# A paired tiling for the last 64 inner rows, loads in halves, elementwise work on GpSimd, and a new total order in an SSM-convolution and Mish kernel on one core

## The chip, the core and the metric

The kernel runs on one core of one Trainium2 chip. A core has TensorE (PE, with its weight loads shown apart as PEld), VectorE (DVE), ScalarE (ACT), GpSimd (POOL) and SyncE (SP), which here only issues transfers. The metric is device time in microseconds. Before the change the median of three runs is 235.5 us (234.25 to 236.78).

## What is computed

Sequence length S = 2048, model width D = 640, inner width F = 1728, all in bf16. With x = A_q:

```python
h  = x + A(layernorm(x), A_k, A_v, A_shift_k, A_ssm_k, A_ssm_D)
h2 = h + B(layernorm(h), B_w1, B_b1, B_w2)

def A(q, k, v, shift_k, ssm_k, ssm_D):
    kv = causal_conv(k, shift_k, taps=4) * v        # along S, per channel
    y  = causal_conv(kv, ssm_k)                     # 2048 taps, by FFT in the reference
    return q * (y + kv * ssm_D)

def B(x, w1, b1, w2):                               # 640 -> 1728 -> 640
    return mish(x @ w1 + b1) @ w2
```

## The kernel before

**Layout.** A token's row index is 16 p + a, with p the partition and a = 0..15; "tile t" is the 128 tokens with a = t. The 640 channels are handled as five groups of 128, and these as three chunks: groups 0 and 1 (chunk 0), 2 and 3 (chunk 1), 4 (chunk 2).

**The long convolution** is done by matrix products as a two-stage transform of length 4096. The steps have names, and most of what follows speaks in these names, with the channel group or chunk first and a running number after it:

- `d_n`, `d_k`, `d_v`, `d_g`, `d_x`: loads of A_ssm_k (five of 0.52 MB), A_k (four quarters of 0.66 MB), A_v (two halves of 1.31 MB), the table G (eight blocks of 0.52 MB) and the rows of A_q. `d_id` loads the table `cst`, which holds the identity for transposes and the first transform's cosines and sines.
- `k1pe`, `k1ev`: transposes of A_ssm_k on TensorE and their eviction from PSUM; `dadd` adds ssm_D to the first tap (a row of one partition).
- `s1kpe`, `s1kev` and `s1vpe`, `s1vev`: first transform stage of the filter and of kv, 16 matmuls of 64 columns each, in pairs (cosine L460, sine L461), and the eviction of 1024 columns.
- `ktpe`, `ktev`, `ktsh`: transposes of A_k (each needs one quarter per step; the fourth step of a group needs the last quarter), eviction, and a shift by one on GpSimd; `wsh`: the short convolution's band matrices on GpSimd (L417); `kspe`, `kv`: the short convolution as matmuls and its product with v on VectorE.
- `s2kpe`, `s2kev` and `s2vpe`, `s2vev`: second stage with G, for the filter (22 pieces) and for kv (8, 8 and 4 pieces). `s2kpe` needs every `s1kev`.
- `sw`: copies of the transformed filter with neighbouring partitions swapped, by transfers from the core's memory to itself; each transfer writes 64 of the 128 partitions.
- `p2`, `p1`: the products in the transformed domain, 128x1024 in bf16, on VectorE. `p2` uses the swapped copy.
- `i1pe`, `i1ev`: first inverse stage; `i2pa`, `i2pb`, `i2pc`: second inverse stage of one tile for the three chunks; `y`: its eviction.

**After the transforms**, per tile: `ln1`, `ln1p` and `lnx` normalise x (statistics on VectorE, a power on GpSimd, the scaled row on ScalarE or GpSimd), `wb` multiplies it with y, `h` adds x, `bn` and `pow` are the second statistics, `hc` centres and scales, `trpe` and `trev` transpose it to the channels' side.

**The inner layer** works in five units of 256, 256, 512, 512, 512 tokens. `m1pe` (L780) makes 256 inner rows of a unit as two blocks of 128, 5 matmuls each over the channel groups; `hb` (L788) applies Mish with the bias from PSUM to `hb`. There are 14 blocks of 128 inner rows for 1728 rows: the last one has 64 rows and is filled up with zeros in w1 (`w1z`), and in w2 (`w2z`). `m2pe` (L798) makes one tile's output, two halves of 320 columns with 14 matmuls each, `res` (L805) adds h, `d_out` writes it.

**The order.** One text, `ORDER`, names every step and its engine (t TensorE, a ScalarE, v VectorE, p GpSimd, d a transfer from SyncE). `_schedule` walks through it and gives each step a slot of its rings: four PSUM tiles of 1024 columns (`R_PS`), and rings for row buffers. Each engine then runs its steps in this order, and a step waits on its engine until its inputs and its slot are there. Durations in `_schedule` only decide the merged order of emission and the slots.

Of the kernel before, what the change touches and what calls it, by code (L numbers as in the profile page):

```python
# [10 lines left out]
ACT = mybir.ActivationFunctionType  # L11
# [15 lines left out]
cz:v d_small:p d_id:d d_n2:d wz:v kz:p wm:t cfpe:t coef:v k1pe2:t d_n0:d k1ev2:v d_n1:d wsh3:p dadd2:v d_n3:d k1pe0:t k1ev0:a dadd0:p k1pe1:t  # L27
s1kpe2_3:t s1kev2_3:a s1kpe2_0:t k1ev1:v s1kev2_0:v dadd1:v s1kpe2_1:t s1kev2_1:a s1kpe2_2:t s1kev2_2:a k1pe3:t k1ev3:v d_k0:d s1kpe1_2:t s1kev1_2:a
s1kpe1_0:t s1kev1_0:v s1kpe0_1:t s1kev0_1:a dadd3:p s1kpe0_0:t d_k1:d s1kpe0_3:t s1kev0_3:v s1kev0_0:a s1kpe0_2:t d_n4:d k1pe4:t k1ev4:v d_x0:d
ln1_0:v s1kev0_2:a s1kpe3_1:t wsh2:p s1kpe3_2:t s1kev3_1:a d_k2:d s1kpe1_3:t s1kev3_2:a ktpe0_0:t ktpe0_1:t dadd4:p s1kpe4_0:t s1kev1_3:a s1kev4_0:a  # L30
s1kpe4_1:t ln1_3:v ktpe0_2:t ln1p3:p wsh0:p d_k3:d s1kev4_1:a ktpe0_3:t ktev0:v s1kpe4_2:t wsh1:p d_v1:d s1kev4_2:a s1kpe4_3:t s1kev4_3:v s1kpe3_3:t
s1kev3_3:a ktsh0:p ln1_1:v d_g2:d s1kpe1_1:t s1kpe3_0:t ktpe1_0:t s1kev3_0:a ktpe2_0:t d_g1:d ktpe1_1:t s1kev1_1:a ln1_2:v ktpe2_1:t ktpe1_2:t d_g5:d
ktpe2_2:t ktpe4_0:t d_g3:d ktpe1_3:t ktev1:v ktpe2_3:t ktev2:a ktpe4_1:t ktpe3_0:t ktpe4_2:t ktsh2:p ktpe4_3:t ktev4:v ktpe3_1:t s2kpe_7:t s2kev_7:a
ktpe3_2:t s2kpe_4:t d_g0:d s2kev_4:a d_a12:d ktpe3_3:t ktev3:v s2kpe_6:t ktsh3:p ktsh1:p d_g4:d kspe0_1:t s2kev_6:a kv0_1:v s2kpe_9:t s2kpe_3:t
kspe3_1:t kv3_1:v s2kev_9:a d_v0:d s2kev_3:a d_g7:d d_g6:d s2kpe_14:t s2kev_14:a kspe2_1:t kv2_1:v s2kpe_13:t s2kev_13:a s2kpe_1:t s2kev_1:a kspe1_1:t
kv1_1:v s2kpe_8:t kspe0_0:t kv0_0:v s2kev_8:a s2kpe_11:t s2kev_11:a s2kpe_0:t s2kev_0:a kspe1_0:t s2kpe_15:t s2kev_15:a kv1_0:v kspe4_1:t kv4_1:v
s2kpe_17:t s2kev_17:a s1vpe0_0:t s1vev0_0:a s1vpe0_2:t ktsh4:p s1vpe1_1:t s2kpe_5:t s1vev0_2:v s2kpe_2:t s1vev1_1:v kspe2_0:t kv2_0:v s2kev_5:a
s2kpe_10:t s2kev_2:a s2kev_10:a sw0_0:d s2kpe_12:t kspe4_0:t s2kev_12:a kv4_0:v s2kpe_18:t s2kev_18:v s2kpe_20:t s2kev_20:a s1vpe2_1:t s1vev2_1:a
kspe3_0:t s2kpe_21:t s2kev_21:a s2kpe_19:t kv3_0:v s2kev_19:a s2kpe_16:t s1vpe1_3:t s1vev1_3:a ln1p0:p s1vpe1_2:t sw1_0:d s1vpe1_0:t s2kev_16:v
s1vev1_0:a s1vpe4_3:t s1vev4_3:a s1vev1_2:v ln1p2:p s1vpe0_1:t s1vev0_1:v s1vpe0_3:t s1vpe3_1:t s1vev3_1:v s1vev0_3:a s1vpe3_3:t s1vev3_3:a s1vpe2_2:t  # L40
s1vev2_2:v s1vpe3_2:t s1vev3_2:a sw0_1:d s2vpe0_1:t s2vpe0_0:t s2vev0_0:v s2vev0_1:a p2_0_1:v p2_0_0:v s2vpe0_2:t s2vev0_2:a s1vpe2_3:t s1vev2_3:a
p2_0_2:v sw1_1:d s2vpe0_3:t s2vev0_3:a s1vpe2_0:t s1vev2_0:a s1vpe3_0:t s1vev3_0:v sw2_1:d s2vpe0_5:t p1_0_2:v s2vpe0_7:t p2_0_3:v s2vpe1_3:t p1_0_1:v
s1vpe4_2:t s1vev4_2:v s2vev0_5:a s2vpe0_6:t s2vev1_3:a s2vev0_7:a p1_0_3:v s2vev0_6:a s1vpe4_0:t s1vev4_0:a s2vpe1_7:t s2vev1_7:a p1_0_0:v s1vpe4_1:t
s1vev4_1:a d_t2m:d s2vpe1_4:t s2vpe1_5:t sw2_0:d s2vpe0_4:t p2_0_7:v p2_0_5:v s2vpe1_0:t s2vev1_5:a s2vev1_0:a p1_0_7:v s2vpe1_6:t s2vev1_6:a p1_0_5:v
s2vev0_4:v s2vev1_4:a s2vpe2_3:t s2vev2_3:a p2_0_6:v s2vpe1_1:t p2_0_4:v p2_1_0:v p1_0_4:v p1_0_6:v p2_1_5:v s2vev1_1:a p2_1_3:v s2vpe1_2:t p2_1_7:v
p2_1_1:v s2vev1_2:a p2_1_2:v s2vpe2_0:t s2vev2_0:a i1pe0_7:t p2_1_6:v i1pe0_0:t i1ev0_0:a s2vpe2_1:t p1_1_1:v p2_1_4:v p1_1_0:v p1_1_5:v p1_1_2:v
p1_1_7:v p1_1_3:v s2vev2_1:a p1_1_4:v p1_1_6:v i1pe0_1:t s2vpe2_2:t d_w12:d i1ev0_7:a d_w13:d i1pe0_5:t i1ev0_1:a i1ev0_5:a p2_2_3:v d_w10:d d_x2:d
p2_2_1:v s2vev2_2:a p2_2_0:v i1pe0_3:t i1pe0_2:t i1ev0_2:a i1pe0_6:t i1ev0_6:a p2_2_2:v p1_2_0:v p1_2_2:v i1pe0_4:t d_w14:d i1ev0_4:a p1_2_1:v
i1pe1_0:t d_w11:d d_w2:d p1_2_3:v w2z:p ln1_15:v i1ev0_3:a ln1p15:p i1ev1_0:a ln1_11:v i1pe1_2:t i1ev1_2:a i1pe1_6:t gate:p lnx3:p i1ev1_6:a i1pe1_7:t
lnx2:p i1pe1_1:t i1pe1_5:t i1ev1_1:a i1ev1_5:v i1ev1_7:a i1pe2_2:t i1ev2_2:a i1pe1_3:t i1ev1_3:a i1pe2_3:t i1ev2_3:a i1pe1_4:t i1ev1_4:a i1pe2_1:t  # L50
# [12 lines left out]
d_out0:d h15:v bn15:v pow15:p i2pb13:t trpe8:t ln1p13:p trev8:v i2pc13:t y13:a m2pe6:t trpe10:t bn14:v pow14:p lnx13:a wb13:v m2pe7:t hc9:v hc11:v
# [784 lines left out]
```

## Time and profile before

| | |
|---|---|
| runs (three) | 234.25, 235.5, 236.78 us |
| profiled execution | 234.49 us, its span 232.7 us |
| mean granted TensorE clock | 0.996 |
| TensorE busy | 220.3 us, 2772 matmuls |
| VectorE busy | 145.7 us, 297 instructions |
| ScalarE busy | 141.2 us, 190 instructions |
| GpSimd busy | 42.9 us, 82 instructions |
| moved by DMA | 28.64 MB, 123 GB/s in the mean |

The span runs from the first to the last instruction; the profiled execution's own time is 1.8 us longer. A matmul's duration in the profile contains its way through the array (a 128-column one is shown with 0.219 us where the next one starts 0.055 us later), so work on TensorE is counted by the distance of starts, not by durations. Line numbers are those of the kernel printed above.

### The profile page before, as it was taken

To read this page: it belongs to the slowest core of one execution; us is meant where nothing else is said; L and a number is where in the kernel's file an instruction comes from. 1 tells how busy PE (TensorE), PEld (TensorE's weight loads), DVE (VectorE), ACT (ScalarE), POOL (GpSimd) and SP (SyncE) were. 2 spreads that over 40 slices of the span, in tenths; PEclk is the share of its full clock that TensorE was granted. 3 is DMA by queue.
4 is the path that set the end of the run, shared out by engine and by line. 5 is a ranking of instruction groups with operands and counts; after the bars stand their busy time and mean duration, and the time that the engine had idled before them with its cause. 6 is when DMAs were issued, how large, how long until landed. Compare 5 with 4: busy or idle time off the path is not lost.

```text
span 232.7 us, 6388 instructions
## 1 busy us (share of the span) xinstructions
PE 220.3 (95%) x2772; PEld 168.4 (72%) x2778; DVE 145.7 (63%) x297; ACT 141.2 (61%) x190; POOL 42.9 (18%) x82
## 2 busy tenths in 40 slices
PE   7898999999888999899999999999999999999993
PEld 2897999998778999689787644677654444677771
DVE  0777978898999995889899679688420000102221
ACT  2498999999999999899961457321307378200000
POOL 3443650000100009214313152231000000000000
PEclk9999999999999999999999999999999999999998
DMA  6999992099991999000000000010300000000312
GB/s 191 373 348 411 412 416 86 4 269 278 267 274 16 341 384 347 28 4 0 3 0 3 30 0 0 3 58 0 116 28 0 0 3 0 0 3 0 111 41 74
DMA packets 19022, 28.64 MB, mean 123 GB/s; under 512 B 1137, under 2 KB 15410, under 8 KB 18610
## 3 DMA queue, kind: packets, MB, share of 16 engines
q1 hardware_dynamic: 18880, 28.23, 34.8%
q8 instruction: 21, 0.34, 0.6%
q14 instruction: 7, 0.06, 0.1%
q0 software_dynamic: 64, 0.00, 0.0%
q10 hardware_dynamic: 50, 0.01, 0.0%
HBM read 20.37 MB, written 2.62 MB: 99 GB/s over the span
## 4 chain that ended last, share of the span: by engine, by line
PE 78%; DMA 7%; DVE 6%; ACT 5%; issue 2%; SPq 1%; ACTq 0%; DVEq 0%
PE ps L798 26%; PE ps L780 26%; ACT uv L367 5%; DMA ra<-in_A_k_dram 4%; PE ps L654 4%; PE ps L653 4%; PE ps L566 3%; DMA rn<-in_A_ssm_k_dram 3%; PE ps L602 2%; PE ps L490 2%; PE ps L751 2%; PE ps L460 2%; PE ps L513 2%; PE ps L713 2%; DVE uk L369 1%
## 5 line engine op out<-in xcount | busy, mean ns | idle before, releaser
L780 PE MATMUL ps<-G 128*128 128x512 bf16 (+1 forms) x344 | 62.3, 336 | 0.3
L798 PE MATMUL ps<-rn,uv 128*128 128x320 bf16 x448 | 62.3, 299 | 0.0
L798 PEld LDWEIGHTS <-uv 128*128 128x128 bf16 x448 | 43.6, 98 | 16.9
L788 ACT ACTIVATE uv<-ps,b1s 128x512 bf16<-128x512 f32 (+1 forms) x70 | 37.2, 604 | 26.1 <-PE ps L780 25.4
L780 PEld LDWEIGHTS <-G 128*128 128x128 bf16 x350 | 33.9, 98 | 24.8 <-issue 0.2
L367 ACT CAST uk<-ps 128x1024 bf16<-128x1024 f32 (+2 forms) x54 | 49.5, 1030 | 3.2 <-PE ps L461 1.9
L805 DVE TENSOR_TENSOR xb<-ps,xb 128x640 bf16<-128x640 f32 x6 | 4.8, 821 | 45.3 <-PE ps L798 45.3
L367 ACT CAST uv<-ps 128x1024 bf16<-128x1024 f32 x30 | 28.2, 1076 | 0.5 <-PE ps L461 0.5
L653 PE MATMUL ps<-a,uv 128*128 128x128 bf16 x160 | 18.3, 219 | 0.0
L653 PEld LDWEIGHTS <-uv 128*128 128x128 bf16 x160 | 17.8, 113 | 0.0
L738 POOL TENSOR_TENSOR r<-ve,mhalf 128x1 f32<-128x1 f32 x16 | 9.0, 565 | 39.1 <-DVE ve L735 39.1
L602 PE MATMUL ps<-uv,G 128*128 128x64 bf16 (+1 forms) x384 | 13.4, 187 | 2.8 <-ACT uv L367 1.5
L692 POOL TENSOR_TENSOR r<-ve,mhalf 128x1 f32<-128x1 f32 x16 | 8.9, 558 | 36.7 <-DVE ve L688 36.7
L602 PEld LDWEIGHTS <-G 128*128 128x128 bf16 x384 | 12.1, 96 | 4.0 <-issue 3.0
L519 DVE TENSOR_TENSOR ra<-ps,rb 128x1024 bf16<-128x1024 f32 x10 | 12.2, 1224 | 1.7 <-PE ps L514 1.7
L369 DVE CAST uv<-ps 128x1024 bf16<-128x1024 f32 x10 | 11.9, 1219 | 1.3 <-ACT uv L367 0.9
L617 DVE TENSOR_TENSOR uv<-uv,uk 128x1024 bf16<-128x1024 bf16 x20 | 12.7, 682 | 0.0
L460 PE MATMUL ps<-cst,ra 128*64 128x128 bf16 x160 | 11.0, 220 | 0.6 <-issue 0.5
L367 ACT CAST rb<-ps 128x640 bf16<-128x640 f32 x13 | 8.4, 705 | 5.2 <-PE ps L713 5.1
L367 ACT COPY G<-ps 128x640 bf16<-128x640 bf16 x7 | 4.9, 693 | 10.9 <-PE ps L751 10.9
L566 PE MATMUL ps<-uk,G 128*128 128x160 bf16 x128 | 11.3, 230 | 0.0
L461 PE MATMUL ps<-cst,ra 128*64 128x128 bf16 x160 | 11.2, 221 | 0.0
(104 smaller groups left out, 354.5 us busy)
## 6 DMA issues: line engine op xcount, KB each, us to landing
G<-tab_g SPq DMA_DIRECT2D x8, 512.0 KB, 11.5
rn<-in_A_ssm_k_dram SPq DMA_DIRECT2D x5, 512.0 KB, 6.3
ra<-in_A_k_dram SPq DMA_DIRECT2D x4, 640.0 KB, 8.3
rb<-in_A_v_dram SPq DMA_DIRECT2D x2, 1280.0 KB, 11.3
G<-in_B_w_dram SPq DMA_DIRECT2D x5, 432.0 KB, 7.2
rn<-in_B_w_dram SPq DMA_DIRECT2D x1, 2080.0 KB, 12.2
rn<-uk SPq DMA_DIRECT2D x4, 512.0 KB, 5.2
rb<-uk SPq DMA_DIRECT2D x8, 256.0 KB, 5.2
```

The source lines that it names most:

```text
L367: nc.scalar.copy(o, i)
L369: nc.vector.tensor_copy(o, i)
L460: nc.tensor.matmul(ps[0:64, dgl, :], lhs, mc, start=True, stop=True)
L461: nc.tensor.matmul(ps[64:128, dgl, :], lhs, ms, start=True, stop=True)
L519: nc.vector.tensor_tensor(kv_w[:, m, :, 8 * h:8 * h + 8, :], rt.tile.rearrange("p (l t d) -> p d t l", l=4, t=8), raw_v[:, 8 * h:8 * h + 8 ...
L566: nc.tensor.matmul(ps[:, o:o + 160], g_v[:, f, :], KA[:, :, f, :], start=True, stop=True)
L602: nc.tensor.matmul(ps[:, fl * st:fl * st + n], g_v[:, f0 + fl, :], V[c.i][:, :, f0 + fl, :], start=True, stop=True)
L617: nc.vector.tensor_tensor(v, v, K[c.i][:, :, f0:f1, :], ALU.mult)
L653: nc.tensor.matmul(pz[:, dgl, :], V[c.i][:, dg // 4, :, dg % 4], a12[:, 0, :], start=True, stop=False)
L780: nc.tensor.matmul(ph[:, i * 512:i * 512 + w], w1[:, dc, fc * P:fc * P + P], lnhT_of(u)[:, dc, 0:w], start=(dc == 0), stop=(dc == NDC - 1))
L788: nc.scalar.activation(hb_of(u)[:, fc, 0:w], rt.tile[:, i * 512:i * 512 + w], ACT.Mish, bias=b1s[:, fc:fc + 1], scale=1.0)
L798: nc.tensor.matmul(po[:, a * 512:a * 512 + 320], hb_of(u)[:, fc, tl * P:(tl + 1) * P], w2[:, fc, a * 320:a * 320 + 320], start=(fc == 0), ...
```

## The change

The order is a new one throughout: every engine gets its steps in another sequence. Its beginning, the part around the second stage, and its end:

```diff
-cz:v d_small:p d_id:d d_n2:d wz:v kz:p wm:t cfpe:t coef:v k1pe2:t d_n0:d k1ev2:v d_n1:d wsh3:p dadd2:v d_n3:d k1pe0:t k1ev0:a dadd0:p k1pe1:t
...
+cz:v kz:p wz:v wm:t d_off:d d_n2:d d_n1:d warm:a d_id:a k1pe2:t k1ev2:v dadd2:v cfpe:t k1pe1:t k1ev1:a d_n0:d k1pe0:t coef:v k1ev0:v s1kpe2_2:t
+dadd0:p s1kev2_2:v d_n4:d d_k2:d s1kpe2_1:t dadd1:p s1kev2_1:a s1kpe2_3:t s1kev2_3:a k1pe4:t s1kpe1_3:t s1kev1_3:a k1ev4:v s1kpe1_0:t s1kev1_0:v
...
+s1kev4_0:v s1kev0_2:a d_k0:d dadd3:p s1kpe3_1:t s1kev3_1:a s1kpe3_2:t s1kev3_2:a s1kpe3_3:t s1kpe3_0:t s1kev3_0:a ktpe3_0:t ktpe3_1:t ln1_3:v d_g1:d
+d_k3:d ktpe3_2:t s1kev3_3:v ktpe2_0:t d_g4:d ktpe3_3:t ktev3:v d_g3:d ktpe2_1:t s2kpe_21:t d_g0:d s2kpe_7:t ktpe2_2:t ktpe2_3:t ktev2:v s2kev_21:a
...
-m2pe14:t res14:v d_out14:d res12:v d_out12:d d_out10:d m2pe9:t res9:v d_out9:d m2pe8:t res8:v d_out8:d d_out11:d m2pe13:t res13:v d_out13:d
...
+d_out10:d resa15:v d_outa15:d m2pe8:t res8:v d_out8:d d_out9:d m2pe13:t res13:v d_out13:d m2pe12:t res12:v d_out12:d res11:v d_out11:d d_out1:d
+m2bpe15:t resb15:v d_outb15:d
```

In the new order A_ssm_k's blocks come as 2, 1, 0, 4 ahead of all else on SyncE, then A_k's third quarter, G's blocks 7 and 2, A_ssm_k's block 3, and the other quarters of A_k with G's block 1 between them. All first-stage products of the filter stand ahead of the transposes of A_k. `warm`, which loads the table for Mish, stands at the start of ScalarE's order, ahead of the load of `cst`, which ScalarE now issues. GpSimd has the steps `p2_0_3`, `p2_0_1`, `p1_0_7`, five `wb`, nine `h`, fifteen of the sixteen `hc`, and eight `lnx` instead of six. Up to the first w1 product 13 tiles of the second inverse stage stand on TensorE; before it was 11 and two of the three parts of a twelfth. The rest of the diff, cut:

```diff
     def emit_small(e):
-        nc.sync.dma_start(cst[:], dram["cst"])
+        nc.scalar.dma_start(cst[:], dram["cst"])
...
-        for _ in range(10):
+        for _ in range(9):
             nc.tensor.matmul(ps[:, 0:512], wz[:, 0:P], wz[:, P:D], start=True, stop=True)
...
     def emit_small2(e):
-        nc.gpsimd.memset(b1b[:], 0.0)
         nc.gpsimd.dma_start(b1b[0:13, :], B_b1[0:13 * P].rearrange("(c p) -> c p", p=P))
-        nc.gpsimd.dma_start(b1b[13:14, 0:64], B_b1[13 * P:FF].rearrange("(c p) -> c p", c=1))
+        for o in (0, 64):
+            nc.gpsimd.dma_start(b1b[13:14, o:o + 64], B_b1[13 * P:FF].rearrange("(c p) -> c p", c=1))
...
     def emit_kn(b):
-        return lambda: nc.sync.dma_start(raw_n[b], A_ssm_k.rearrange("(d m l) s -> m d l s", m=NDC, l=4)[b])
+        v = A_ssm_k.rearrange("(d m l) s -> m d l s", m=NDC, l=4)[b]
+
+        def fn():
+            for d in range(0, 32, 16):
+                nc.sync.dma_start(raw_n[b][4 * d:4 * d + 64], v[d:d + 16])
+        return fn
...
             def fn(e, f0=f0, f1=f1, c=c, which=0):
+                eng = nc.gpsimd if e == "pool" else nc.vector
                 v = V[c.i][:, :, f0:f1, :]
                 if which == 0:
-                    nc.vector.tensor_tensor(v, v, K[c.i][:, :, f0:f1, :], ALU.mult)
+                    eng.tensor_tensor(v, v, K[c.i][:, :, f0:f1, :], ALU.mult)
                     return
...
-    w1_z = OP("w1z", ("pool", 0.4), s2_pes + s2k_pes, emit=lambda e: nc.gpsimd.memset(w1[:, :, FF:FP], 0.0), prio=6)
...
-        nc.sync.dma_start(w2[0:64, 13, :], B_w2[13 * P:FF, :])
-    w2_z = OP("w2z", ("pool", 0.6), i1_pes[0], emit=lambda e: nc.gpsimd.memset(w2[64:P, 13, :], 0.0), prio=7)
+        for i in range(2):
+            nc.sync.dma_start(w2[64 * i:64 * i + 64, 13 + i, :], B_w2[13 * P:FF, :])
+    def emit_w2z(e):
+        nc.gpsimd.memset(w2[64:P, 13, :], 0.0)
+        nc.gpsimd.memset(w2[0:64, 14, :], 0.0)
...
         def wbf(e, lnx_rt=lnx_rt, tt_rt=tt_rt):
-            nc.vector.tensor_tensor(tt_rt.tile, tt_rt.tile, lnx_rt.tile, ALU.mult)
+            (nc.gpsimd if e == "pool" else nc.vector).tensor_tensor(tt_rt.tile, tt_rt.tile, lnx_rt.tile, ALU.mult)
...
                 for i in range(2):
                     fc = fp * 2 + i
+                    if fc == NFC - 1:
+                        for dc in range(NDC):
+                            for o in (0, 64):
+                                nc.tensor.matmul(ph[o:o + 64, 512:512 + w // 2], w1[:, dc, fc * P:FF], lnhT_of(u)[:, dc, o * w // P:(o + 64) * w // P],
+                                                 start=(dc == 0), stop=(dc == NDC - 1))
+                        continue
...
+                    n = w // 2 if fc == NFC - 1 else w
+                    nc.scalar.activation(hb_of(u)[:, fc, 0:n], rt.tile[:, i * 512:i * 512 + n], ACT.Mish, bias=b1s[:, fc:fc + 1], scale=1.0)
...
-                        nc.tensor.matmul(po[:, a * 512:a * 512 + 320], hb_of(u)[:, fc, tl * P:(tl + 1) * P], w2[:, fc, a * 320:a * 320 + 320],
+                        o = tl * P
+                        x = 1 if fc == NFC - 1 and o >= w // 2 else 0
+                        nc.tensor.matmul(po[:, a * 512:a * 512 + 320], hb_of(u)[:, fc, o - x * w // 2:o - x * w // 2 + P], w2[:, fc + x, a * 320:a * 320 + 320],
                                          start=(fc == 0), stop=(fc == NFC - 1))
...
+            for a in range(2):
+                o_pe2 = OP(f"m2{'ab'[a]}pe{t2}", ("pe", 1.905), hbs + [d_w2, w2_z, o_pe2], allocs=[] if a else [rt], uses=[rt] if a else [], emit=(lambda e, f=pe2, a=a: f(e, cols=(a,))), prio=100 + u + 0.5)
```

`h` and `hc` get the same choice of engine as `wb`. For the last 64 inner rows, the first half of a unit's tokens now goes to partitions 0 to 63 of the block and the second half to partitions 64 to 127, each with half as many columns; w2 holds the last 64 rows twice, once over zeros and once under zeros, and the bias of these rows is loaded twice. The second product keeps its 28 matmuls of 320 columns per tile. Only tile 15 is cut: `m2ape15` makes its left 320 columns, four tiles run, and `m2bpe15` makes the right ones, with a residual and an output each. `_schedule`'s own durations and waits change too, which moves nothing by itself.

## The prediction

> **What bounds the kernel now.** I read the busy table by slices first, then the work of each engine in stretches of 10 us, then the order of time on ScalarE and on the weak places, and last the chain of waits from 100 us on.
>
> ```profile
> PE   7898999999888999899999999999999999999993
> DVE  0777978898999995889899679688420000102221
> ACT  2498999999999999899961457321307378200000
> DMA  6999992099991999000000000010300000000312
> ```
>
> One digit is 5.8 us. TensorE (PE) is near full everywhere, ScalarE (ACT) only up to slice 16, the DMA engines up to slice 6. Stretches (start:end, then busy us and count of PE, PE weight loads, DVE, ACT, POOL, then clock, DMA share, GB/s):
>
> ```profile
> 20.00:30.00 10.00, 8.65 (x184) 8.21 (x179) 8.28 (x17) 8.73 (x10) 5.96 (x6) 1.00 1.02 411
> 60.00:70.00 10.00, 8.46 (x238) 7.57 (x235) 9.92 (x17) 10.00 (x12) 0.63 (x1) 1.00 0.94 268
> 70.00:80.00 10.00, 8.98 (x220) 8.98 (x219) 10.00 (x24) 10.00 (x12) 0.00 (x0) 1.00 0.48 155
> 100.00:150.00 50.00, 49.89 (x383) 35.54 (x383) 42.55 (x123) 32.90 (x60) 15.11 (x30) 1.00 0.02 5
> ```
>
> So there are three stages. Up to about 29 us the loads bind. From there to 93 us it is ScalarE: in order of time its evictions run from 29.74 to 92.97 us with four pauses, 0.26, 0.16, 0.46 and 0.27, together 1.15 us, 68 casts at a pitch of 0.92:
>
> ```profile
> 29.74 11.95 ACT L367 CAST uk<-ps 128x960 bf16<-128x960 f32 x13 [0.34 <-PE ps L566]
> 54.91 19.34 ACT L367 CAST uv<-ps 128x1024 bf16<-128x1024 f32 x21 [0.46 <-PE ps L461]
> 79.60 12.09 ACT L367 CAST uk<-ps 128x1024 bf16<-128x1024 f32 x13
> ```
>
> From the first product with w1 at 100.86 us to 228.8 TensorE never stops. Pieces of the chain (start, us, what):
>
> ```profile
> 105.82 2.18 PE ps L780 x20
> ...
> 137.38 2.16 PE ps L780 x10
> ...
> 198.36 30.44 PE ps L798 x224
> 228.82 0.82 DVE xb L805
> ```
>
> A 512-wide matmul thus takes 0.216 us, a 256-wide one 0.109, a tile of the second product 30.44/8 = 3.80.
>
> **The last 64 inner rows.** Per unit, 5 matmuls of full width become 5 pairs of half width, two 64-column tiles side by side. That two such tiles run at once is seen in the transform stage, where a new pair starts each 0.055 us, the time of 128 columns once (128 x 0.216 / 512 = 0.054):
>
> ```profile
> 10.16 0.22 PE L460 MATMUL ps<-cst,x 128*64 128x128 bf16 x1
> 10.16 0.22 PE L461 MATMUL ps<-cst,x 128*64 128x128 bf16 x1
> 10.21 0.22 PE L460 MATMUL ps<-cst,x 128*64 128x128 bf16 x1
> 10.22 0.22 PE L461 MATMUL ps<-cst,x 128*64 128x128 bf16 x1
> ```
>
> A 512 unit saves 5 x 0.108 = 0.54, a 256 unit 5 x 0.0545 = 0.27: 3 x 0.54 + 2 x 0.27 = 2.17 us. Each goes into and out of the narrow tiling, 10 changes; where nothing waits, the next matmul in the trace starts about 0.092 late at such a change (0.08 to 0.11 in some 15 places). 10 x 0.092 = 0.92. Net -1.25, all on the path. The order of the transform stage makes 14 such changes instead of 26, 1.1 us, which I count at nothing, since ScalarE hides it. The shorter activations (0.69 to 0.48) and the second zeroing of w2 lie beside other work; so do one warm-up matmul less (0.43) and the bias loads, three issues of 0.5 to 0.76 on GpSimd's queue, moved behind p1_0_7 and some 20 us ahead of their use.
>
> **Start.** SyncE issues the A_ssm_k halves at once, ten issues for five of 0.55 to 0.70, at 0.33 to 0.7 each (the bounds are the rows of its shortest issues and of the whole loads; it has free time after 3 us, since it then waits for landings); cst goes to ScalarE's queue behind a 1.28 us table load and the 0.2 us warm activation, so at about 2.3 us instead of 0.72; with its 2.2 us to landing it is there at 4.5, and the first transposes run at 5.9 in before. If sharing the engines with the halves eats that 1.4 us, each further 0.1 costs 0.1 there, but 25.5 us below hides it. The other table load, 1.28 at 102 us, goes, where the Mish groups wait 25.4 us for PE anyway: nothing.
>
> **When ScalarE's long stretch begins.** The first s2k product follows the transposes of the last A_k quarter, which PE waited for until 22.15 us. Ahead of that quarter and with it came 6.0 MB; now three blocks of G (g7, g2, g1) come before it, 1.57 MB more. At 0.41 MB/us (20 to 30 us) that is 3.8 us, less 0.4 for the earlier start: 25.5 us. But by then all of the s1k work has been done: 20 groups of 0.44 and five transposes of 1.08 fit into 5.9 to 22, and the last of their evictions, on VectorE behind x0 and two statistics of 1.23, ends near 25.5 too. So s2k evictions start at 26.1 instead of 29.74. ScalarE then has 21 x 0.92 + 0.37 + 47 x 0.925 + one lnx 0.82 = 64.0 us to the last i1 eviction, plus the same pauses, 1.15: 91.25 instead of 92.97, -1.7. Ends: no gain if the pauses double and the start is 27; -4 if the G blocks overlap better.
>
> VectorE's load up to its last product rises by 1.8 us by the rows (three more evictions of 1.14, one more statistic of 1.23, less three products of 0.60 and small ones), and in before it is through at 85.35 after 13 us of waits, 6 us ahead of the last transposes; that is the cover. Late loads: A_v's second-issued half is needed by the sixth kv product at about 39 us and ends at 12.3 MB; the last G block (12.85 MB) is used by s2k_15 at 26.1 + 0.4 + 16 x 0.92 = 41; in before 12.8 MB were in by 36 us. The swap copies wait for the eighteenth s2k eviction, 26.1 + 16.5 = 42.6, and went out at 45.6; a12 and t2m, now behind them all, are used after 65 us. The three products given to GpSimd: 128x1024 at the rate of L417 (2058 ns for 1120) 1.88, at that of the copy L499 (608 ns for 508) 1.23; I take L417, also two-input. The three run beside PSUM evictions, which GpSimd does not disturb (L369's 1.22 us copy at 7.15, under L417, is as long as any). Without that cover:
>
> ```profile
> 7.09 2.06 POOL L417 TENSOR_TENSOR hc<-cst,coef 128x1120 bf16<-128x1120 bf16 x1 [4.21 <-DVE coef L409]
> ...
> 8.41 0.83 DVE L543 TENSOR_TENSOR x<-x,rn 1x128 bf16<-1x128 bf16 x1
> ```
>
> This VectorE instruction takes 0.21 elsewhere; here it ends 0.09 after GpSimd's does. Two-input work of the two excludes each other. Two memsets of w2 (0.63 each) also stand on GpSimd's queue ahead of the last of the three products, which the first i1 product needs some 8 us later.
>
> **Into the products.** From the last i1 eviction to the first w1 product it was 7.9 us, with PE idle 0.38 and 1.23 in it while the chain y, gate, residual, statistics, pow, centring ran. Now 13 inverse tiles (0.537 each) instead of 11 and 0.8 of a twelfth fill it: the stretch stays about 8, and 1.2 x 0.537 = 0.65 us of work is gone from behind it. -0.65.
>
> **GpSimd in the second half.** It gets 15 centrings (0.87 by L702, the nearest row), 9 residuals and 5 gates (1.18 by L417), 2 more lnx. The tightest place is tile 7: from h3 on GpSimd's queue to hc7 holds 4 two-input steps, 6 pow, 6 centrings, 5 ln1p, 3 lnx: 4.7 + 3.4 + 5.2 + 4.1 + 2.6 = 20 us. Meanwhile PE has 15.1 of first products, 11.4 of second ones, 2.8 of transposes and inverse tiles: 29 us. 9 us of cover; I take nothing, bounds 0 and +3.
>
> **Tail.** The last residual is half as wide: 0.82 to about 0.45. But res12, res11 and then three outputs, at 0.33 each, are now queued ahead of it on VectorE and SyncE inside the last 1.9 us, and a landing takes 1.8. -0.1, bounds -0.4 and +0.6.
>
> **Sum** on the profiled execution (234.49 us, span 232.7, so 1.8 lie around it): -1.7 - 0.65 - 1.25 - 0.1 = -3.7, so 230.8. The median of the runs, 235.5, stands 1.0 above that execution; the same saving from it would be 231.8.
>
> **Rivals.** (1) *The half loads are slow.* Each half reaches 64 partitions. The nearest rows are the swap copies, also 64 partitions each: 268 to 279 GB/s at 94 to 98% busy engines, against 411 for the 128-partition loads; but they read and write the core's memory, so they don't settle it. 2.62 MB of A_ssm_k take 6.4 us at 411, 9.7 at 270, 12.7 if half the partitions give half the rate. The last A_k quarter comes as much later and ScalarE's stretch with it: +3.3, 234.1, or +6.3, 237.1, slower than before. It decides from 3.7 us of delay on, below 260 GB/s. The Trainium skill, "SBUF — State Buffer", section "Can I just issue two DMAs to hit both halves?", says that two transfers into the two partition halves do not add up (+6% over one), and its table has 196 against 328 GB/s; by that ratio the load would take 10.7 and the sum be 235.1. No trace here shows such a pair. (2) *GpSimd's hold on two-input work makes VectorE the bound* in the product stage: 3 x 1.88 waited out in full and 1.8 of load more are 7.4 against 6 us of cover, +1.4, and the same waits make a centring late by the 3 of the bound above: 235.2. Against it stands that each product is placed beside evictions. (3) *The pairs don't run side by side* when they accumulate: 2.17 is lost, 233.0. For it, only that the transform's pairs don't accumulate. (4) *ScalarE starts earlier:* -4 for -1.7, and half of its pauses gone: 230.8 - 2.3 - 0.6 = 227.9. PE's 1.13 us wait at 21 us is for a load alone, which speaks for it.
>
> **Numbers.** Forecast 0.50, 230.8 with 228.5 to 233; rival (1) 0.28; (2) 0.10; (3) 0.05; (4) 0.07. 1% of 234.5 is 2.3, about what a measurement can tell: 232.1 and 236.8 bound "same". Faster: 0.45 of the forecast, 0.02 of (1), 0.02 of (2), 0.01 of (3) and (4) whole, 0.57. Same: 0.05 + 0.13 + 0.04 + 0.03 = 0.25. Slower: 0.13 of (1), 0.04 of (2), 0.01 of (3), 0.18. The range 227 to 237 leaves out some 0.03 below and 0.12 above; the forecast's own is the one given with it.
>
> **What would show it.** s2k evictions on ScalarE from about 26 us, the last i1 eviction near 91, the first w1 product near 99; a paired group of five at 0.54 us plus twice 0.09; GpSimd busy about 80 us (42.9 + 13 + 16.5 + 5.6 + 1.7); no PE pause after the first product. Loads below 300 GB/s before 12 us and an A_k quarter landing after 28 us would show (1). A PE pause on a centring would make the second half's zero wrong.

## The result, and the profile after

| | before | changed |
|---|---|---|
| median of the runs shown beside each other (us) | 236.1 (4 runs, 234.3 to 237.8) | 253.6 (4 runs, 252.9 to 253.7) |
| ratio, 95% interval | | 1.074 (1.065 to 1.082) |
| span of the profiled execution (us) | 232.7 | 251.9 |
| first transposes of the normalised tiles (us) | 98.8 | 105.7 |
| first product with w1 (us) | 100.8 | 109.3 |
| TensorE's last matmul ends, by the distance of starts (us) | 228.6 | 248.3 |
| GpSimd busy (us) | 42.9 | 110.6 |

The kernel became 17 us slower, where 230.8 was forecast. Two executions at a granted clock near 0.6, one of the kernel before and one of a variant, took about 370 us and enter no ratio given here. 8.5 us are lost ahead of the first w1 product and 11.2 behind it. The changed kernel's span in 40 slices of 6.3 us shows where, in the same rows as before, with GpSimd's (POOL) and the granted clock's:

```profile
PE   6997899988779899598978399999997999999994
DVE  0597897889999999787694628413323000101223
ACT  2278799998979988356913134723223457112000
POOL 0080086007900045559989997997964000000000
PEclk9999999999999999889999689999999999999999
DMA  6999991399926992000000000000030000000122
```

Counted from 0, TensorE, which used to be full from slice 17 on, has holes at slices 16 and 22, GpSimd is at seven tenths or more from slice 18 to 28, and behind both holes the clock that TensorE is granted falls. The same by stretches (start:end, then busy us and count of PE, PE weight loads, DVE, ACT, POOL, then clock, DMA share, GB/s):

```profile
60.00:70.00 10.00, 7.59 (x211) 6.50 (x205) 9.93 (x11) 9.57 (x12) 8.99 (x9) 1.00 0.96 286
...
100.00:110.00 10.00, 7.03 (x63) 5.92 (x62) 7.21 (x18) 4.98 (x9) 4.73 (x5) 0.83 0.01 2
110.00:120.00 10.00, 8.76 (x91) 7.39 (x89) 8.05 (x28) 6.14 (x14) 9.40 (x10) 1.00 0.00 0
...
140.00:150.00 10.00, 6.57 (x38) 4.40 (x40) 4.79 (x14) 2.91 (x4) 9.23 (x11) 0.67 0.01 2
```

In the last two of these stretches GpSimd is the busiest engine. The groups of GpSimd (busy us, mean ns of one, then idle time) say with what:

```profile
L759 POOL TENSOR_SCALAR hc<-xa,mv,r 128x640 bf16<-128x640 bf16 x6 | 15.4, 2562 | 0.3
...
L740 POOL TENSOR_TENSOR rb<-rb,ra 128x640 bf16<-128x640 bf16 x5 | 7.2, 1431 | 2.8 <-ACT rb L372 2.8
...
L718 POOL TENSOR_SCALAR ra<-x,r,nmr 128x640 bf16<-128x640 bf16 x3 | 2.6, 876 | 0.0
```

A centring (L759) takes 2.5 us, where the prediction took 0.87 for it, the time of the norm ahead of the gate (L718, in the kernel before L702): the same engine, shape and type, also with two per-partition operands. The row of before is

```profile
L702 POOL TENSOR_SCALAR ra<-x,r,nmr 128x640 bf16<-128x640 bf16 x4 | 3.4, 867 | 0.0
```

The 15 centrings sum to 37.9 us, not 13. TensorE's waits name the same line (engine, line, releaser: total us, times, longest):

```profile
PEld L767 <- POOL hc L759: 14.9, 8, 4.4
...
PE ps L767 <- POOL hc L759: 12.7, 8, 4.3
```

And in the chain of waits (start, us, what) the worst pause, 4.43 us up to 143.38, is four steps of one queue, with a gate of a later tile (`rb`) standing between two centrings (the last of them is tile 7's):

```profile
136.10 2.51 POOL hc L759
138.61 0.53 POOL r L754
139.14 1.36 POOL rb L740
140.50 2.84 POOL hc L759
143.38 0.71 PE ps L767 x5
```

### The profile page after: what moved, and what is told of

Same layout as the page of the kernel before. It is cut to its first block, busy times and chain, and to the rows that moved or that the text cites. A ratio compares the mean times of both kernels' runs of the same rounds, so it can differ in the third digit from the quotient of the medians.

```text
span 251.9 us, 6466 instructions
## 1 busy us (share of the span) xinstructions
PE 224.0 (89%) x2795; PEld 169.6 (67%) x2802; DVE 142.2 (56%) x267; ACT 135.5 (54%) x185; POOL 110.6 (44%) x117
## 4 chain that ended last, share of the span: by engine, by line
PE 38%; DVE 21%; POOL 19%; DMA 11%; issue 7%; ACT 1%; POOLq 1%; SPq 1%; DVEq 0%
PE ps L823 17%; POOL hc L759 10%; PE ps L802 9%; DMA ra<-in_A_k_dram 4%; DVE uv L630 4%; DMA rn<-in_A_ssm_k_dram 4%; PE ps L578 3%; DMA rn<-uk 3%; POOL r L754 3%; DVE rb L740 2%; DVE rn L634 2%; DVE uv L374 2%; PE ps L501 2%; DVE rb L634 2%; DVE st L749 1%
## 5 line engine op out<-in xcount | busy, mean ns | idle before, releaser
L802 PE MATMUL ps<-G 128*128 128x512 bf16 (+1 forms) x318 | 58.2, 336 | 0.7 <-ACT uv L811 0.4
L802 PEld LDWEIGHTS <-G 128*128 128x128 bf16 x325 | 31.3, 98 | 23.3 <-issue 1.1
L829 DVE TENSOR_TENSOR xa<-ps,xa 128x640 bf16<-128x640 f32 x6 | 4.9, 825 | 41.0 <-PE ps L823 41.0
L767 PE MATMUL ps<-cst,hc 128*128 128x128 bf16 x80 | 7.5, 237 | 12.7 <-POOL hc L759 12.7
L829 DVE TENSOR_TENSOR xb<-ps,xb 128x640 bf16<-128x640 f32 (+1 forms) x7 | 4.9, 726 | 20.1 <-PE ps L823 20.1
L767 PEld LDWEIGHTS <-hc 128*128 128x128 bf16 x80 | 5.3, 106 | 15.3 <-POOL hc L759 14.9
L759 POOL TENSOR_SCALAR hc<-xa,mv,r 128x640 bf16<-128x640 bf16 x6 | 15.4, 2562 | 0.3
L759 POOL TENSOR_SCALAR hc<-xb,mv,r 128x640 bf16<-128x640 bf16 x6 | 15.0, 2506 | 0.2
L614 PEld LDWEIGHTS <-G 128*128 128x128 bf16 x384 | 11.5, 96 | 4.6 <-issue 4.4
L708 POOL TENSOR_TENSOR r<-ve,mhalf 128x1 f32<-128x1 f32 x16 | 8.9, 557 | 10.8 <-DVE ve L704 10.8
L374 DVE CAST uk<-ps 128x1024 bf16<-128x1024 f32 x10 | 12.0, 1220 | 0.6 <-PE ps L472 0.3
```

What stands on the lines that cost most here:

```text
L374: nc.vector.tensor_copy(o, i)
L614: nc.tensor.matmul(ps[:, fl * st:fl * st + n], g_v[:, f0 + fl, :], V[c.i][:, :, f0 + fl, :], start=True, stop=True)
L759: (nc.gpsimd if e == "pool" else nc.vector).tensor_scalar(hc_rt.tile, xt(t2), mv2[:, t2, 0:1], r2[:, t2:t2 + 1], ALU.subtract, ALU.mult)
L767: nc.tensor.transpose(pt[:, dc * P:(dc + 1) * P], hc_rt.tile[:, dc * P:(dc + 1) * P], ident)
L802: nc.tensor.matmul(ph[:, i * 512:i * 512 + w], w1[:, dc, fc * P:fc * P + P], lnhT_of(u)[:, dc, 0:w], start=(dc == 0), stop=(dc == NDC - 1))
```

## The experiments

All times are medians beside runs of the kernel before on the same chip, whose medians were 234.7 to 235.0.

**The centring back on VectorE.** In the order, the letter of 15 steps:

```diff
-hc0:p ... hc2:p hc3:p ... hc15:p
+hc0:v ... hc2:v hc3:v ... hc15:v
```

> The changed kernel with its 15 GpSimd centrings back on VectorE, at the same places of the order; nothing else. Theory A: the loss is the centring itself, which GpSimd takes 2.53 us for (0.45 on VectorE), so that TensorE waits 12.7 us for it and is granted a clock of 0.83 and 0.67 after two of the pauses, some 3 us more. Then 253.6 falls to 236 to 241, the pauses ahead of the transposes (L767) shrink below 4 us, GpSimd's busy time falls from 110.6 to about 73, and the first w1 product, at 109.3 now, comes about 2 to 3 us earlier. Theory B (three products on GpSimd hold VectorE up) and theory C (the half loads delay the start) both leave the second half as it is: no less than 250.

Measured 241.7 (241.5 to 242.1), 0.7 above the range given. GpSimd was busy 72.7 us; TensorE's idle time from 100 us to its last matmul fell from 13.4 to 4.4 us, and the first w1 product came 2.4 us earlier. So the centring on GpSimd is 12 us of the loss.

**The centring on GpSimd in another form.**

```diff
-gpsimd.tensor_scalar(hc, x, mean, r, ALU.subtract, ALU.mult)
+gpsimd.tensor_scalar(nmr2, mean, r, -1.0, ALU.mult, ALU.mult)
+gpsimd.tensor_scalar(hc, x, r, nmr2, ALU.mult, ALU.add)
```

> The 15 centrings stay on GpSimd but are written as x times r plus (minus mean times r), the form that the norm ahead of the gate uses on GpSimd at 0.87 us; the product of mean and r is one more 128x1 step of 0.30 ahead of each. Theory A1: it is the form (subtract first, then multiply) that costs 2.53; then each centring with its small step takes 1.17, GpSimd is busy 20 us less (about 90), and the time falls by most of the 12.7 us of pauses, to 240 to 246. Theory A2: what costs is this tile or this place on GpSimd, whatever the form: it stays at 2.5, the small steps add 4.5 us to GpSimd, 254 to 258.

Measured 240.6 (240.3 to 240.9), GpSimd busy 89.9, a centring 0.87. It is the form, not the engine, that cost 13 us (253.6 less 240.6).

**The three products back on VectorE.**

```diff
-p2_0_3:p ... p2_0_1:p ... p1_0_7:p
+p2_0_3:v ... p2_0_1:v ... p1_0_7:v
```

> The three gating products that went to GpSimd are back on VectorE, at the same places of the order. Theory B: one VectorE product took 2.61 us instead of 0.68 beside one of them, another 1.26; VectorE wins 2.5 us of waits and gets 1.8 us of work, and its last product, which ends at 91.5 now, ends 1 to 3 us earlier, with the time at 250.5 to 252.5. Theory A: the second half is untouched and hides nothing of it, so at most that 1 us is seen: 252.5 to 254.

Measured 252.9 (252.7 to 253.0): 0.7 less. The hold that the prediction named is there, in the changed kernel's VectorE in order of time:

```profile
59.57 1.29 DVE L630 TENSOR_TENSOR uv<-uv,uk 128x1024 bf16<-128x1024 bf16 x2
60.77 2.61 DVE L634 TENSOR_TENSOR rn<-rn,uv 128x1024 bf16<-128x1024 bf16 x1
63.31 2.34 DVE L374 CAST uv<-ps 128x1024 bf16<-128x1024 f32 x2
```

One product takes 2.61 instead of 0.68, ending half a microsecond after GpSimd's product, which ran from 60.31 to 62.84; the next held one takes 1.26. But VectorE must do the three itself when it gets them back, 1.8 us, so little was to be won.

**Whole loads.**

```diff
-for d in range(0, 32, 16):
-    nc.sync.dma_start(raw_n[b][4 * d:4 * d + 64], v[d:d + 16])
+nc.sync.dma_start(raw_n[b], v)
```

> The five A_ssm_k blocks are loaded whole (128 partitions each) as in the kernel before, the rest of the change stays. Theory C: between 3 and 12 us the queue moved 234 to 265 GB/s where it later moves 390 to 430; whole loads bring the last A_k quarter in at about 25.5 instead of 27.9 us and the time falls by up to 2.4, to 251.2 to 252.5. If VectorE's products bound that stage instead, the 2.4 us are hidden and the time stays within 0.8 of 253.6, though the quarter lands earlier.

Measured 251.2, but from 249.7 to 253.0. The rate is beyond doubt. Stretches of the changed kernel, then of this one (the last number is GB/s):

```profile
3.00:6.00 3.00, 2.43 (x6) 0.60 (x4) 0.00 (x0) 0.00 (x0) 0.00 (x0) 1.00 1.07 277
6.00:9.00 3.00, 2.75 (x24) 2.48 (x25) 0.83 (x1) 0.00 (x0) 0.00 (x0) 1.00 1.04 254
9.00:12.00 3.00, 2.91 (x48) 2.60 (x48) 1.94 (x7) 1.73 (x1) 0.00 (x0) 1.00 1.02 243
```

```profile
3.00:6.00 3.00, 3.00 (x14) 1.52 (x13) 0.00 (x0) 0.00 (x0) 0.00 (x0) 1.00 1.04 364
6.00:9.00 3.00, 2.63 (x35) 2.32 (x34) 2.10 (x6) 0.49 (x1) 0.00 (x0) 1.00 0.99 392
9.00:12.00 3.00, 3.00 (x74) 2.84 (x72) 2.46 (x3) 2.58 (x3) 0.91 (x3) 1.00 1.00 409
```

With all DMA engines busy in both (the number before the rate), half loads move two thirds as much. In SyncE's order the last A_k quarter landed at 27.8 us in the changed kernel and at 24.5 with whole loads, 3.4 us earlier. What of it reaches the end is less sure: the span of the profiled execution fell by 1.5 us, the median by 2.4. In that profile TensorE's pause at 20.5 us grew to 2.41, the clock was 0.83 from 20 to 30 us, and ScalarE's long stretch began at 28.12 instead of 28.80. At the same mean clock, 0.993, two executions with whole loads took 249.7 and 250.2 us and two of the changed kernel 252.9 and 253.6: 3.3 us, though only two against two.

**All three together** (multiply and add, products on VectorE, whole loads).

> The three repairs together: centring on GpSimd as multiply and add, the three products back on VectorE, whole A_ssm_k loads; the pairs, the tail in halves, GpSimd's gates and residuals and the new order stay. If the three costs lie one after another on the path, 240.6 less 0.7 less 2.4 gives 237.5 (236.5 to 238.5). If they hide each other (theory D: VectorE bounds the stage of the products whatever comes before), 239 to 240.6. Either way it stays above the kernel before by 2 us or more, since VectorE's stretch from its first to its last product remains some 4 us longer than it was.

Measured 237.1 (235.9 to 238.9), ratio 1.010 (1.006 to 1.013). The three costs add up: 253.6 - 13.0 - 0.7 - 2.4 = 237.5. ScalarE's long stretch now begins here (one group of ScalarE in order of time):

```profile
26.49 12.57 ACT L373 CAST uk<-ps 128x320 bf16<-128x320 f32 x14 [0.43 <-PE ps L574]
```

That is the 26.1 of the prediction; in the changed kernel it was 28.80.

**The pairs alone, in the kernel before.** Of the change only the pairs, w2's second copy of the last 64 rows and that of their bias, in the old order:

```diff
+if fc == NFC - 1:
+    for dc in range(NDC):
+        for o in (0, 64):
+            nc.tensor.matmul(ph[o:o + 64, 512:512 + w // 2], w1[:, dc, fc * P:FF], ...)
+    continue
```

> The kernel before with the paired column tiles alone: its own order, loads and engines; last 64 inner rows as two 64-column tiles, the second copy of their rows of w2 and of their bias, zeros beside it. The step of the prediction: -2.17 of matmuls plus 10 changes of tiling at 0.09 make -1.25, so a ratio of 0.995 (0.993 to 0.998), with a paired group of five at 0.67 to 0.76 us, tiling changes included, where five full matmuls take 1.08. If the pairs ran one after another, the group would take 1.26 and the ratio be 1.004.

Measured 234.0, ratio 0.997 (0.994 to 0.9997), where 0.995 was expected; from the first w1 product to the last matmul 126.8 us instead of 127.8. A unit of 512 in TensorE's order of time:

```profile
142.81 2.32 PE L791 MATMUL ps<-G 128*128 128x512 bf16 x10
145.06 0.74 PE L787 MATMUL ps<-G 128*64 128x256 bf16 x10
145.73 1.53 PE L812 MATMUL ps<-rn,uv 128*128 128x320 bf16 x10
```

Ten half-width matmuls from 145.06 to 145.73: 0.67 us from start to next start, so they run side by side, and the group starts 0.09 late (142.81 + 10 x 0.216 = 144.97). 0.76 in all, by the prediction 0.72.

**Three evictions from VectorE back to ScalarE**, beside the three repairs.

```diff
-s2vev1_7:v ... s2vev1_4:v ... i1ev1_3:v
+s2vev1_7:a ... s2vev1_4:a ... i1ev1_3:a
```

> The kernel with the three repairs, and with three of the evictions that the new order gives to VectorE in the product stage (two of the second v transform of chunk 1, one of the first inverse step) back on ScalarE, at the same places of the order. Theory D: from its first product to its last VectorE does seven evictions of 1.15 us, three in the kernel before, and never waits there; without three of them its last product ends 2.3 to 3.4 us earlier, and the time falls by 1.5 to 3 against the kernel with the three repairs. Rival: ScalarE takes 0.92 more for each, 2.8 us, and pauses only 3.6 us in that stage in all, not always where it is needed; then the gain is under 0.7.

Measured 236.7, ratio 1.009 (1.006 to 1.012), against 1.010 without: not to be told apart. VectorE's last product did end 2.4 us earlier (85.9 instead of 88.3), but ScalarE now runs without any pause from 53.95 us on,

```profile
53.95 21.20 ACT L373 CAST uv<-ps 128x1024 bf16<-128x1024 f32 x23 [0.86 <-PE ps L610]
...
77.50 14.15 ACT L373 CAST uk<-ps 128x1024 bf16<-128x1024 f32 x15
```

and its last inverse eviction ends at 93.3 instead of 94.1. The rival was right: ScalarE is full in this stage, and what VectorE gains there it loses in part to two new waits (1.24 and 0.84 us).

**The centring in four forms, by tile.**

```diff
-gpsimd.tensor_scalar(hc, x, mean, r, ALU.subtract, ALU.mult)
+(hc, x, mean, r, ALU.subtract, ALU.mult), (hc, x, -mean, r, ALU.add, ALU.mult),
+(hc, x, r, mean * r, ALU.mult, ALU.subtract), (hc, x, r, -mean * r, ALU.mult, ALU.add)
```

> The changed kernel with the GpSimd centring written in four forms, by tile: as it is (subtract the mean, multiply by r) for tiles 4, 8 and 12 and 0; add minus the mean, multiply by r; multiply by r, subtract mean times r; multiply by r, add minus mean times r. All have two per-partition operands in f32 and the same tile. Theory A1a: a subtraction costs: the first and the third form take 2.5, the others 0.87. Theory A1b: the order costs (another operation than the multiplication first): first and second 2.5, third and fourth 0.87. Theory A1c: only multiply and add is short: 2.5, 2.5, 2.5 and 0.87. The time of this kernel says nothing more: 242 to 252.

GpSimd in order of time, tiles 4 to 7 (subtract then multiply; add then multiply; multiply then subtract; multiply then add):

```profile
127.58 2.51 POOL L763 TENSOR_SCALAR hc<-xa,mv,r 128x640 bf16<-128x640 bf16 x1
...
131.82 0.87 POOL L766 TENSOR_SCALAR hc<-xa,nmr,r 128x640 bf16<-128x640 bf16 x1
...
133.69 2.52 POOL L769 TENSOR_SCALAR hc<-xa,r,nmr 128x640 bf16<-128x640 bf16 x1
...
138.79 0.88 POOL L772 TENSOR_SCALAR hc<-xa,r,nmr 128x640 bf16<-128x640 bf16 x1
```

The subtraction costs it, first or second; the order of the two operations does not matter, and the third and the fourth form have the same operands. The other tiles show the same to 0.02 us.

**The first tiles on VectorE**, beside the three repairs and the three evictions.

```diff
-wb1:p ... hc0:p
+wb1:v ... hc0:v
```

> The kernel with the three repairs and the three evictions on ScalarE, and of GpSimd's work two steps more back on VectorE, at the same places of the order: the gate of tile 1 and the centring of tile 0. Theory E: ahead of the first w1 product TensorE pauses 1.93 us for this chain: the residual of tile 0 on VectorE takes 1.58 instead of 0.48, since GpSimd's gate of tile 1 (1.65) runs beside it, and the centring on GpSimd takes 0.27 + 0.87 against 0.45 on VectorE. Without both, the chain is 1.1 + 0.7 less 0.45 for the gate on VectorE: TensorE's pause falls to 0.4 to 0.8, the first w1 product comes 1.1 to 1.5 us earlier, and so does the end: 235.2 to 235.6. If something else holds the first tiles (the statistics, the power on GpSimd), less than 0.5 is won.

Measured 236.3, ratio 1.007 (1.004 to 1.010). The pause fell from 1.93 only to 1.35 us, the first w1 product came 0.55 earlier: half of theory E's gain or less, and the times (236.7 without this step) are not to be told apart.

**Everything on VectorE**, beside the three repairs and the three evictions.

```diff
-hc0:p ... wb1:p ... h3:p ...
+hc0:v ... wb1:v ... h3:v ...
```

> The kernel with the three repairs and the three evictions on ScalarE, and all centrings, gates and residuals on VectorE, at the same places of the order: GpSimd keeps what it had before the change. Theory F: GpSimd's help in the second half is worth nothing, since VectorE does the same work 3 times as fast (0.45 for 0.87 + 0.28, 0.48 for 1.40) and is 30 of 40 us busy there, while one GpSimd queue makes tiles 4 to 7 late by 1.8 us: the pauses at 98 and at 128 us fall below 0.6 each, and the time to 233.0 to 234.5, below the kernel before. Theory G: VectorE's load (12 us more in its busiest 50) makes new pauses: 236 or more.

Ratio 1.017 (1.011 to 1.023); five executions took 238.0 to 241.4 us, the middle one 238.2. That is slower than the kernel before, against theory F, and than the 236.7 with GpSimd's help. Where the time goes is read from the last run below.

**The kernel before with pairs and tail in halves.**

```diff
-m2pe13:t res13:v d_out13:d
+m2ape13:t resa13:v d_outa13:d m2bpe13:t resb13:v d_outb13:d
```

> The kernel before with the paired column tiles and with its last tile's second product, residual and output in halves of 320 columns; nothing else. From TensorE's last matmul to the end of the span it is 4.1 us in the kernel before and 3.6 in the changed one, so the halves are worth 0.5, not the 0.1 of the prediction; with the pairs' 1.3 by the profile the span is 230.9 (230.4 to 231.4), and the ratio 0.992 to 0.995. If the halves win 0.1 or nothing, the span stays at 231.4 or above.

Ratio 0.994 (0.991 to 0.997), inside the range given but not to be told apart from the pairs alone; the span, 231.9, lies above its range. So nothing is shown to be won by the halves. TensorE at the end:

```profile
223.77 2.20 PE L812 MATMUL ps<-rn,uv 128*128 128x320 bf16 x15
226.55 2.06 PE L812 MATMUL ps<-rn,uv 128*128 128x320 bf16 x14 [0.58 <-DVE xb L817]
```

Between the halves TensorE pauses for the first half's residual. From its end to the span's it is 3.45 us instead of 4.05; the pause of 0.75 takes that back.

**The same with another product between the halves.**

```diff
-m2pe8:t res8:v d_out8:d d_out11:d m2ape13:t resa13:v d_outa13:d m2bpe13:t
+m2ape13:t m2pe8:t resa13:v d_outa13:d res8:v d_out8:d d_out11:d m2bpe13:t
```

> The kernel before with pairs and tail in halves, where the last second product's first half now runs one product earlier (its two halves have the product of tile 8 between them, as the changed kernel has others between them). In the kernel with the halves next to each other TensorE paused 0.75 us at 225.8, behind the first half's residual on VectorE, since both halves lie in one tile of PSUM. Theory H: that pause took back the 0.6 that the shorter tail won (3.45 instead of 4.05 us from TensorE's end to the span's); without it the span is 230.6 to 231.1 and the ratio 0.991 to 0.994. If the halves are worth nothing in themselves, the ratio stays at the 0.997 of the pairs alone.

Measured 233.2, ratio 0.992 (0.988 to 0.996): the lowest median of all kernels here. The pause is gone and TensorE's end is 3.5 us from the span's. The profiled execution itself misses its forecast (233.1): its first half ran about 2 us later, at a clock of 0.97 from 40 to 100 us; the middle span of the twelve executions is 231.4, also a little above the 230.6 to 231.1. The interval overlaps that of the pairs alone, so the half microsecond of the tail rests on the two profiles.

**One gate less on GpSimd**, beside the first tiles' two steps.

```diff
-wb11:p
+wb11:v
```

> The kernel with the first tiles' two steps on VectorE, and of GpSimd's gates one more, that of tile 11, on VectorE too. Theory I: TensorE's pause of 1.75 us at 127 us is the centring of tile 7, which stands on GpSimd's queue behind this gate (1.40), as the centring that took 2.84 stood there at 140 us in the changed kernel. Without it the pause falls to 0.2 to 0.5 and the end comes 1.2 to 1.5 us earlier: 234.8 to 235.2, level with the kernel before. If GpSimd's queue as a whole is what is late (six steps of centring, power and norm before it), another step takes its place and under 0.5 is won.

Measured 234.7, ratio 0.998 (0.995 to 1.002), level with the kernel before, and 1.6 below the kernel without this step, as theory I has it. In the kernel with the three evictions GpSimd's order of time had shown that gate in front of tile 7's centring:

```profile
126.47 1.40 POOL L736 TENSOR_TENSOR rb<-rb,ra 128x640 bf16<-128x640 bf16 x1
127.84 0.61 POOL L756 TENSOR_SCALAR nmr<-mv,r 128x1 f32<-128x1 f32 x1
128.55 0.87 POOL L757 TENSOR_SCALAR hc<-xa,r,nmr 128x640 bf16<-128x640 bf16 x1
```

With it gone no pause over 0.45 us is left behind 100.1 us. GpSimd is busy 78.6 us, near the 80 that the prediction named, but by another sum: the three products are not on it here.

**Everything on VectorE, again**, the same kernel.

> The kernel with all centrings, gates and residuals on VectorE once more, for a profile at full clock: it took 238 to 240 where the same kernel with GpSimd's help took 236.5. Theory G: VectorE is then busy throughout from the last products to the end of the second unit and TensorE pauses there on VectorE's residuals, statistics or centrings, over 4 us after 96 us where the kernel with help has 3.1. Theory G2: the loss lies before 96 us, where nothing was changed, and is chance: then the time comes out at 236 to 237 this time.

238.2 again in two executions, ratio 1.011 (1.003 to 1.019). Up to the first w1 product it is as early as the kernel with the first tiles on VectorE (102.2 us against 102.0), so G2 is out. Then TensorE pauses on VectorE's centrings, 1.54, 1.50, 0.56 and 0.47. Theory G is right in these pauses; busy throughout VectorE is not (7.8 to 9.6 of each 10 us from 100 to 150). VectorE in order of time ahead of the first of these:

```profile
105.05 0.89 DVE L745 BATCH_NORM_STATS2 st<-x 128x6 f32<-128x320 bf16 x2
...
106.28 0.88 DVE L698 BATCH_NORM_STATS2 st<-xa 128x6 f32<-128x320 bf16 x2
...
107.51 0.80 DVE L759 TENSOR_SCALAR hc<-x,mv,r 128x640 bf16<-128x640 bf16 x2
```

The order was written with the centring on another queue: on VectorE it stands behind the next tile's statistics and a set for a tile of a later unit, 1.2 us each, and each engine runs its steps in the order written.

## Why the prediction was wrong, step by step

**The step that failed: "15 centrings (0.87 by L702, the nearest row)".** In the section on GpSimd's second half this term was 13 us for tiles that TensorE waits for, under 9 us of cover. Measured, it is 37.9 us. For tile 7, the place named as tightest, the six centrings took 15.4 us (five of 2.51, one of 2.84) instead of 5.2, and GpSimd's stretch from h3 to the end of hc7 took 33.8 us (109.55 to 143.32) instead of 20. So the cover is gone there, as the pause up to 143.38 shows. "I take nothing" was thus wrong by 13.0 us, the difference that the form alone makes (240.6 for 253.6); 2.2 us of it lie ahead of the first w1 product. The row was the nearest one in engine, shape, type and number of operands, but not in the operation: multiply and add, where the centring subtracts. Its bounds were 0 and +3; the farther row of the same engine, L417's two-input rate, would have given 1.18 and not 2.5 either. No row of the trace of before had a subtraction on GpSimd; so the bound from above should have been wide, and 15 instructions on one queue make even a doubling of 0.87 the largest unknown of the change.

**The cover itself, "29 us".** It was too large as well. Ahead of tile 7's transposes the new order has two second products on TensorE, not the three that "11.4 of second ones" counts. In the kernel with multiply and add TensorE's work beside that stretch is 25.1 us (107.08 to 133.97, less a pause of 1.75), while GpSimd needs 26.0 (107.87 to 133.91), since gates, residuals and norms take longer there than the sum has them (a residual 1.39 to 1.62 for 1.18) and each centring has a small step of 0.26 beside it. So even with centrings of 0.87 there was no cover at tile 7. The 1.75 us are what was left of the pause, until one gate was taken off that queue.

The Trainium skill, "GPSIMD Engine Reference", section "Engine selection", calls GpSimd's one-input elementwise work roughly line-rate and does not set operations apart. The traces do: for 640 elements of each partition multiply and add takes 0.87 us, twice VectorE's 0.45 for its centring, and the subtraction 2.51, more than five times as long.

**"A PE pause on a centring would make the second half's zero wrong."** The prediction named this sign, and it came: 12.7 us of such pauses.

**ScalarE's stretch, -1.7.** Its start was estimated well for whole loads (26.1; 26.49 in the kernel with three repairs), but in the changed kernel it is 28.80. The gain behind it failed for another reason: "in before it is through at 85.35 after 13 us of waits, 6 us ahead of the last transposes; that is the cover". Those 13 us of VectorE's waits lie ahead of 57 us. Between its first product and its last (57.2 to 85.4 us before) VectorE never waited; the new order gives it five evictions of 1.15 us there instead of three (seven in the kernel with the three repairs, whose first product starts at 54.3), holds of 2.5 us, three products of 0.6 less, and a first product 1.8 us later: 2.3 + 2.5 - 1.8 + 1.8 = 4.8 of the 6.1 us by which its last product came later (91.5 for 85.4). The last inverse eviction came at 97.2, not at 91.25. Three evictions given back to ScalarE won nothing measurable, so moving work between these two engines did not get the 1.7.

**Rival (1), half loads.** Its rate was nearly right (270 GB/s assumed, 243 to 277 measured, 364 to 409 whole), and so was its delay of the last A_k quarter (3.3 us; measured 3.4 against whole loads in the same order, though it landed at 27.8 and not after 28). Its price, 3.3 us, is 2.4 by the medians and 3.3 by the executions at equal clock. It was given 0.28 as the whole of the outcome; it came as one of three. The swap copies, the nearest rows, had the rate, and the prediction left it beside the sum rather than in it. The Trainium skill, "SBUF — State Buffer", section "Can I just issue two DMAs to hit both halves?", says that transfers into the two halves do not add up. By the page's table (196 against 328 GB/s) the ratio is 0.60; the trace agrees, with 0.59 to 0.76 in the six stretches above.

**Rival (2), GpSimd's hold on two-input work.** The hold is real (2.61 for 0.68; later a residual of 0.48 takes 1.57 beside a gate of 1.58). Its price is 0.7 us for the three products, half of the 1.4 assumed.

**The pairs, -1.25.** Right: -1.0 by the profile, 0.997 (0.994 to 0.9997) by the runs; rival (3) is out.

**The earlier inverse tiles, -0.65.** Not confirmed: the stretch from the last inverse eviction to the first w1 product, said to stay at 8 us, was 12.1 us. The form of the centring explains 2.2 us of this (the first w1 product came at 107.1 with multiply and add), wb1 and hc0 on GpSimd another 0.55; the rest was not taken apart.

**The tail, -0.1.** Too small by the profiles: -0.45 to -0.6 (from 4.05 us to 3.6 in the changed kernel and 3.5 in the best one), as long as something stands between the halves.

**The sum.** With the three repairs, the three evictions and the three steps taken off GpSimd, the new order comes to 234.7, not to 230.8. It contains pairs and tail, which bring the kernel before to 233.2. So the rest of the order (another start, the evictions' places, GpSimd's help) costs about 1.5 us by the medians instead of winning 2.35. The first w1 product at 102.3 for 100.8 shows that it is lost ahead of that point; from there to the last matmul both kernels take 126.8 to 126.9 us. Step by step, of the 8.5 us lost ahead of that product the three repairs take back 5.9 (103.5), the three evictions and the first tiles 1.5 (102.0). Of the 11.2 lost behind it the other form of the centring takes back 10.5 (128.4 us to the last matmul instead of 139.0), the one gate 1.5. Which of the order's many moves costs the rest was not taken apart further.

## What to carry to other kernels

A duration is borrowed from a row with the same operation, not only the same engine and shape; where no such row exists, the bound is wide, and when the step is repeated on one in-order queue ahead of the busiest engine, it is worth a look of its own. Cover is counted in the stretch where the work falls, not over the whole stage: 13 us of idle time ahead of the first product hid nothing behind it. An order belongs to the engines that it was written for: the same step moved to a faster engine at the same place came later, not earlier (tile 2's centring ended at 107.95 us on VectorE and at 106.3 on GpSimd).

## What was not expected of the hardware

On GpSimd a 128x640 bf16 operation with a tensor and two per-partition operands takes 0.87 us as multiply and add, in either order, and 2.5 us as soon as one of the two is a subtraction. (In the changed kernel two norms in the multiply-and-add form took 1.18 and 1.74; why was not looked into.) On VectorE the subtracting form takes 0.45.

The two longest pauses of the changed kernel, 3.12 and 4.43 us, were each followed by a lower granted clock: 0.83 and 0.67 in their stretches of 10 us. The length of one pause does not decide it. With whole loads the clock was 0.83 from 70 to 80 us behind a pause of 1.62, and so it was in the kernel with the turned tail behind one of 1.70; in the changed kernel it was 1.00 there behind one of 1.61, and in the kernel with the three repairs it stayed 1.00 behind 2.13. What decides is not shown. By the two stretches of the changed kernel 10 x 0.17 + 10 x 0.33 = 5 us of TensorE's full rate are lost, part of it while TensorE was idle anyway. Its times do not show them: four executions with mean clocks of 0.973, 0.980, 0.993 and 0.993 took 253.6, 253.7, 253.6 and 252.9 us.

A half load cost SyncE as long to issue as a whole one (0.59 us against 0.60 in the median). Eight of them followed each other at 0.85 us from start to start: the sixth and the seventh began only at 4.66 and 6.12, just behind the landings of the first two at 4.64 and 6.10.
